# One gate form for all tokens, left-over rows through a scratch tensor, and a table that places the work

## The chip, the cores and the metric

The kernel runs on one core of a Trainium2 chip. That core has five engines with instruction queues of their own: TensorE (PE, matmuls; its weight loads are shown apart as PEld), VectorE (DVE), ScalarE (ACT), GpSimd (POOL) and SyncE (SP), which here issues most DMA transfers. Each queue runs in order; an instruction that waits for another engine holds up what is behind it on its own queue. The metric is the device time of one execution in microseconds.

## The reference

Two parts in a row. Attention packs 576 tokens of each of 8 heads into 32 with `p`, and attends back to them; the result is the input of a feed-forward block with the gate h * erf(softplus(h)).

```
def _attn_ref(q, k, v, p):
    scale = 1.0 / np.sqrt(q.shape[-1])
    def sm_attn(qq, kk, vv):
        s = scale * np.matmul(qq, kk.transpose(0, 1, 3, 2))
        s = s - np.max(s, axis=-1, keepdims=True)
        a = np.exp(s)
        a = a / (np.sum(a, axis=-1, keepdims=True) + 1e-09)
        return np.matmul(a, vv)
    p_packed = sm_attn(p, k, v)
    return sm_attn(q, p_packed, p_packed).astype(np.float32)

def _moe_ref(x, w_in, w_out):
    h = x @ w_in
    sp = np.maximum(h, 0.0) + np.log1p(np.exp(-np.abs(h)))
    g = h * erf(sp)
    return (g @ w_out).astype(np.float32)
```

q, k and v are 8 x 8 x 576 x 64 (batch, heads, tokens, width), p has 32 tokens, w_in is 512 x 2048 and w_out 2048 x 512. The two weights are 64-bit floats, which the kernel turns into 32-bit floats itself by shifting bits.

## The kernel before, in words

The attention's output is never formed. For each batch b the second attention's weights (576 tokens by 8 heads of 32, `a2`) and w' = packed values times w_in (`w_prime`, four blocks j of 512 columns) are made, and h = w' times a2. Float32 operands are split into a high and a low part of type fp32r, and a product is three matmuls (high x high, low x high, high x low).

The work is cut into 128 units (b, f): f is one of 16 blocks of 128 hidden columns. Units go (0, f 0-7), (1, f 0-7), (0, f 8-15), (1, f 8-15), then batches 2 to 7 whole, f 0 to 15. Unit 8 is thus (1, 0), and unit 32 is (2, 0). For a unit:

- `h_block` makes h of 128 columns by 576 tokens in two halves of 288 tokens, six matmuls each (line 308), into PSUM banks of `ps_h`, of which there are two. ScalarE copies each half into `hs` (L311 or L313).
- The gate has two forms. Units 0 to 31 are grouped by three (`gate_group`): Softplus for three units (L286), Erf for three (L289), and a product on VectorE (L291). Softplus, Erf and Exp need different function tables, so a switch costs an ACT_TABLE_LOAD. Units from 32 on use a form of three Tanh and a Square on ScalarE (L321 to L326) and three operations on VectorE (L324 to L327), which share a table with Exp.
- `split_g` makes gh (L272) and gl (L273) on VectorE, two buffers each, and POOL copies the last 64 of the 576 tokens away into `rh` and `rl` (L279).
- `o_block` multiplies with w_out: four blocks of 128 tokens, three matmuls each (L345), summed over f in four PSUM banks. It runs 3 units behind h (5 in the grouped part).
- The 64 left-over tokens of two batches together fill 128 rows; `o_rest` multiplies them in 48 matmuls (L369) once for each pair of batches, from `rh` and `rl`.

The attention of the next batch (twelve stages of a generator, with `ps_m`, a single PSUM buffer), the w' blocks, and the conversions of the weights (`load_f32`: a DMA into one of two staging buffers `wst`, one ScalarE and three VectorE instructions, L92 to L95; w_out is split too, L108 and L109) are put between the units by rules that spread them over a stretch (`plan`). Within what the code issues, a scheduler orders each engine's instructions by its own estimate of time; only the ScalarE functions that need tables are chained in the order written (`in_turn`), and those in the grouped part alone.

## Time and profile before

| what | us |
|---|---|
| three runs: median, lowest, highest | 808.8, 806.19, 4030.56 |
| the profiled execution, its own time | 806.4 |
| its span, from the first instruction to the last | 804.6 |
| mean granted TensorE clock, share of full | 0.949 |

The profile is of one execution. A row of a group of instructions gives its line, engine, operation, output <- inputs, shapes and count, then the busy time, the mean of one in ns, and the idle time of the engine just before them with what ended it. A row of a stretch gives its bounds, its length, each engine's busy time with the count of instructions, the granted clock, the DMA share and GB/s. In the timeline and the chain of waits a row starts with its start and its length. Since matmuls are pipelined, the busy time of one (393 ns for 512 columns) is longer than its share of the queue: twelve in a row take 2.74 us.

### The profile page before, as it was taken

To read this page: it belongs to the slowest core of one execution; us is meant where nothing else is said; L and a number is where in the kernel's file an instruction comes from. 1 tells how busy PE (TensorE), PEld (TensorE's weight loads), DVE (VectorE), ACT (ScalarE), POOL (GpSimd) and SP (SyncE) were. 2 spreads that over 40 slices of the span, in tenths; PEclk is the share of its full clock that TensorE was granted. 3 is DMA by queue.
4 is the path that set the end of the run, shared out by engine and by line. 5 is a ranking of instruction groups with operands and counts; after the bars stand their busy time and mean duration, and the time that the engine had idled before them with its cause. 6 is when DMAs were issued, how large, how long until landed. Compare 5 with 4: busy or idle time off the path is not lost.

```text
span 804.6 us, 12933 instructions
## 1 busy us (share of the span) xinstructions
PE 742.4 (92%) x5008; PEld 579.1 (72%) x5008; DVE 575.8 (72%) x876; ACT 578.1 (72%) x938; POOL 132.2 (16%) x270
## 2 busy tenths in 40 slices
PE   4458738999999999999999999999999999999996
PEld 1237505878867787778877786778877786878885
DVE  3787697845476558978797559777797559768654
ACT  3369367968577767879697657889697658878764
POOL 0002101211031212211211021112221021211101
PEclk8569957999999999999999999999999999999999
DMA  9633543202240512002300321011400310000002
GB/s 309 235 124 107 179 145 126 100 1 102 75 110 1 102 53 93 1 6 97 132 1 1 115 75 58 0 60 43 132 1 3 110 60 1 1 27 28 1 1 66
DMA packets 26685, 57.98 MB, mean 72 GB/s; under 512 B 3072, under 2 KB 4096, under 8 KB 26624
## 3 DMA queue, kind: packets, MB, share of 16 engines
q1 hardware_dynamic: 25472, 55.06, 20.8%
q0 software_dynamic: 1152, 2.10, 1.6%
q8 instruction: 39, 0.64, 0.3%
q14 instruction: 22, 0.18, 0.1%
HBM read 45.61 MB, written 11.53 MB: 71 GB/s over the span
## 4 chain that ended last, share of the span: by engine, by line
PE 83%; DMA 6%; DVE 6%; ACT 4%; issue 1%; SPq 0%; DVEq 0%; ACTq 0%
PE o L345 42%; PE h L308 25%; PE or L369 5%; PE wp L258 5%; DMA wi<-w_in 2%; PE p L213 2%; DMA v<-v 2%; PE s L180 1%; PE s L227 1%; DMA wos<-w_out 1%; PE t L201 1%; DVE wo L94 1%; DVE wpl L261 1%; DVE wo L95 1%; DVE w_in_sb L94 0%
## 5 line engine op out<-in xcount | busy, mean ns | idle before, releaser
L345 PE MATMUL o<-woh,gl 128*128 128x512 f32 x512 | 201.2, 393 | 0.0
L345 PE MATMUL o<-wol,gh 128*128 128x512 f32 x512 | 200.7, 392 | 0.0
L345 PE MATMUL o<-woh,gh 128*128 128x512 f32 x512 | 173.1, 398 | 0.4 <-DVE gh L272 0.4
L308 PE MATMUL h<-a2h,wph 128*128 128x288 f32 x512 | 158.5, 310 | 12.3 <-ACT hs L311 8.3
L308 PE MATMUL h<-a2h,wpl 128*128 128x288 f32 x512 | 153.5, 300 | 0.0
L308 PE MATMUL h<-a2l,wph 128*128 128x288 f32 x512 | 153.4, 300 | 0.0
L279 POOL CAST rh<-gh 128x64 fp32r<-128x64 f32 x128 | 61.7, 483 | 531.8 <-DVE gh L272 531.8
L308 PEld LDWEIGHTS h<-a2h,wph 128*128 128x128 f32 x512 | 97.8, 191 | 47.0 <-ACT hs L311 10.3
L313 ACT ACTIVATE hs<-h 128x288 f32<-128x288 f32 x192 | 75.7, 406 | 71.8 <-PE h L308 68.4
L345 PEld LDWEIGHTS o<-woh,gh 128*128 128x128 f32 x512 | 93.7, 189 | 29.7 <-issue 4.8
L345 PEld LDWEIGHTS o<-woh,gl 128*128 128x128 f32 x512 | 96.1, 188 | 21.1 <-DVE t L325 1.8
L345 PEld LDWEIGHTS o<-wol,gh 128*128 128x128 f32 x512 | 96.1, 188 | 20.3 <-issue 2.2
L327 DVE SCALAR_TENSOR_TENSOR hs<-t,hs 128x576 f32<-128x576 f32 x96 | 72.5, 755 | 49.6 <-ACT t L326 48.5
L273 DVE TENSOR_TENSOR gl<-hs,gh 128x576 fp32r<-128x576 f32 x128 | 101.0, 789 | 7.3 <-POOL rh L279 0.5
L308 PEld LDWEIGHTS h<-a2l,wph 128*128 128x128 f32 x512 | 98.2, 192 | 7.2 <-DVE a2l L248 1.9
L308 PEld LDWEIGHTS h<-a2h,wpl 128*128 128x128 f32 x512 | 98.1, 192 | 2.7 <-issue 2.6
L326 ACT ACTIVATE t<-t,bias 128x576 f32<-128x576 f32 x96 | 74.1, 772 | 32.5 <-DVE t L325 32.1
L272 DVE CAST gh<-hs 128x576 fp32r<-128x576 f32 x128 | 58.3, 456 | 53.6 <-PE o L345 48.3
L324 DVE SCALAR_TENSOR_TENSOR t<-t,hs 128x576 f32<-128x576 f32 x96 | 72.0, 751 | 19.9 <-ACT u L323 19.7
L279 POOL CAST rl<-gl 128x64 fp32r<-128x64 f32 x128 | 64.8, 507 | 116.6 <-DVE gl L273 91.4
L321 ACT ACTIVATE t<-hs,bias 128x576 f32<-128x576 f32 x96 | 74.9, 780 | 2.2
L322 ACT ACTIVATE t<-t,bias 128x576 f32<-128x576 f32 x96 | 74.5, 776 | 2.0
(74 smaller groups left out, 926.7 us busy)
## 6 DMA issues: line engine op xcount, KB each, us to landing
k<-kT SPq DMA_DIRECT2D x32, 288.0 KB, 4.2
q<-qT SPq DMA_DIRECT2D x32, 288.0 KB, 4.4
wi<-w_in SPq DMA_DIRECT2D x16, 512.0 KB, 4.8
v<-v SPq DMA_DIRECT2D x32, 256.0 KB, 4.0
wos<-w_out SPq DMA_DIRECT2D x16, 512.0 KB, 3.8
out<-ob SPq DMA_DIRECT2D x32, 256.0 KB, 2.2
out<-ob POOLq DMA_DIRECT2D x8, 256.0 KB, 5.7
v<-v SPq DMA_DIRECT2D x8, 128.0 KB, 4.2
```

Source lines behind the costliest of these rows:

```text
L258: nc.tensor.matmul(ps[NK * c:NK * c + NK, r, :], pt[b][64 * r:64 * r + 64, NK * c:NK * c + NK], w_in_sb[64 * r:64 * r + 64, c, j * FB:(j + ...
L272: nc.vector.tensor_copy(ghi[:], hs[:])
L273: nc.vector.tensor_tensor(glo[:], hs[:], ghi[:], op=ALU.subtract)
L279: nc.gpsimd.tensor_copy(kept[:, f % PER, b % 2, :], g[:, NTB * P:S])
L308: nc.tensor.matmul(ps[:, 0:HT], w[:, r, fo:fo + P], a[:, r, at_c], start=(m == 0), stop=(m == 5))
L313: nc.scalar.mul(hs[:, at_c], ps[:, 0:HT], 0.5)
L321: nc.scalar.activation(t[:], hs[:], AF.Tanh, bias=bias[:, 0:1], scale=2.0 * T_SCALE)
L322: nc.scalar.activation(t[:], t[:], AF.Square, bias=bias[:, 1:2], scale=Q_SCALE)
L324: nc.vector.scalar_tensor_tensor(t[:], t[:], 0.5 * A2, hs[:], op0=ALU.mult, op1=ALU.add)
L326: nc.scalar.activation(t[:], t[:], AF.Tanh, bias=bias[:, 3:4], scale=2.0 * A_SCALE)
L327: nc.vector.scalar_tensor_tensor(hs[:], t[:], 1.0, hs[:], op0=ALU.add, op1=ALU.mult)
L345: nc.tensor.matmul(acc[b][x][:], gg[:, x * P:(x + 1) * P], w[:], start=(first and n == 0), stop=(last and n == 2))
```

## The change

- The gate has one form, Softplus and Erf, for all 128 units, in groups of four (three near the start and at the end in other sizes: `ends`). All table functions, Exp of the attention too, are chained in the order written. The program has 86 table loads in place of 28.
- POOL's copies of the left-over tokens go. Each gh and gl is stored by a DMA on SP into `rest`, a tensor in device memory (128 rows of 256 bytes), and `o_rest` loads a block of 512 KB of it into a staging buffer `wst` for every 12 matmuls. gh and gl have three buffers.
- A table (`PLAN`) says behind which unit each stage of the attention, each w' block and each conversion stands. h comes in halves with half of another unit's o between them; o is due `wait` units behind the end of its group, one unit's o for each unit of h.
- From unit 48 on, each TensorE instruction is chained to the one before (`pe`), so TensorE runs in program order.
- At the start, the first block of w_in comes in two loads of 1 MB into a part of `w_in_sb` that is not used yet, maxima and Exp of batch 0 read PSUM directly, and batch 1's p, k, v and q are loaded ahead of the second block of w_in, into buffers of w_out among others.

```diff
+PLAN = {
+    "att": {1: (1, 1, 2, 2, 3, 4, 4, 5, 5, 7, 7), 2: (15, 15, 19, 19, 20, 20, 22, 24, 25, 25, 25, 27, 28, 30)},
+    "steady": (0, 0, 0, 1, 2, 2, 5, 6, 7, 9, 11, 11, 12, 13),
...
+    "ends": (4, 5, 8, 12, 13, 16),
+    "wait": (4, 1, 1, 1, 1),
+    "strict": 48,
+}
...
+    def pe(ins):
+        if strict[0] and pe_last:
+            tc.add_manual_dep(ins.ins, pe_last[-1], mybir.DependencyInfo(
+                mybir.DependencyClass.NoSync, mybir.DependencyReason.DATA), reason="order")
+        pe_last[:] = [ins.ins.name]
...
     def split_g(hs, b, f):
...
-        for kept, g in zip(rest[pair, k], (ghi, glo)):
-            nc.gpsimd.tensor_copy(kept[:, f % PER, b % 2, :], g[:, NTB * P:S])
+        for x, g in enumerate((ghi, glo)):
+            nc.sync.dma_start(rest[b // 2, f // PER, :, x, f % PER, b % 2, :], g[:, NTB * P:S].bitcast(F32))
...
-    def h_block(b, f, n):
+    def h_part(n, c):
...
-            if grouped:
-                nc.scalar.copy(hs[:, at_c], ps[:, 0:HT])
-            else:
-                nc.scalar.mul(hs[:, at_c], ps[:, 0:HT], 0.5)
+        nc.scalar.copy(hs[:, at_c], ps[:, 0:HT])
+        if c == 0:
             return
-        nc.scalar.activation(t[:], hs[:], AF.Tanh, bias=bias[:, 0:1], scale=2.0 * T_SCALE)
-        nc.scalar.activation(t[:], t[:], AF.Square, bias=bias[:, 1:2], scale=Q_SCALE)
-        nc.scalar.activation(u[:], t[:], AF.Tanh, bias=bias[:, 2:3], scale=U_SCALE)
-        nc.vector.scalar_tensor_tensor(t[:], t[:], 0.5 * A2, hs[:], op0=ALU.mult, op1=ALU.add)
-        nc.vector.scalar_tensor_tensor(t[:], u[:], 0.5 * A1, t[:], op0=ALU.mult, op1=ALU.add)
-        nc.scalar.activation(t[:], t[:], AF.Tanh, bias=bias[:, 3:4], scale=2.0 * A_SCALE)
-        nc.vector.scalar_tensor_tensor(hs[:], t[:], 1.0, hs[:], op0=ALU.add, op1=ALU.mult)
+        group.append((hs_of.pop(n), b, f))
+        if n + 1 in ends:
+            gate_group()
+            closed.append(n)
...
     def o_rest(pair, k):
...
-        g = rest.pop((pair, k))
+        g = spool.tile([P, 2, PER, 2 * TAIL], F32R, name=f"g{pair}_{k}", tag="wst")
+        nc.sync.dma_start(g[:].bitcast(F32), rest[pair, k].rearrange("p x i two t -> p x i (two t)"))
...
+    for m, (b, f, first, last) in enumerate(units):
+        wait = PLAN["wait"]
+        sent_at = max(sent_at + 1, close[m] + wait[min(m // G, len(wait) - 1)])
+        here = parts.setdefault(min(sent_at, N + m), [])
+        here += [(o_part, (b, f, first, last, x)) for x in (1, 2, 3, 0)]
+        if b % 2 and f == NF - 1:
+            here += [(o_rest, (b // 2, k)) for k in range(NFB)]
+    for n in range(N + NF):
+        strict[0] = n >= PLAN["strict"]
+        here = parts.get(n, [])
+        some = (len(here) + 1) // 2
+        if n < N:
+            h_part(n, 0)
+        for block, what in here[:some]:
+            block(*what)
+        if n < N:
+            h_part(n, 1)
+            do(plan.pop(n, []))
+        for block, what in here[some:]:
+            block(*what)
```

Three places show how instructions move. A name like gl0_7 is gl of batch 0, f 7; wi3_2 is the staged w_in block of columns 3, rows 2; the last number is only a mark of the program.

VectorE around gl of batch 0's unit 7, before:

```order
L291 TENSOR_TENSOR hs0_6_789<-t0_6_935,hs0_6_789 128x576
L95 SCALAR_TENSOR_TENSOR w_in_sb_87<-wi3_3_1041,w_in_sb_87 128x512
L291 TENSOR_TENSOR hs0_7_865<-t0_7_937,hs0_7_865 128x576
L272 CAST gh0_6_945<-hs0_6_789 128x576
L291 TENSOR_TENSOR hs1_0_918<-t1_0_939,hs1_0_918 128x576
L93 TENSOR_SCALAR wo12_1106<-wo12_1106 128x512
L272 CAST gh0_7_952<-hs0_7_865 128x576
L273 TENSOR_TENSOR gl0_6_946<-hs0_6_789,gh0_6_945 128x576
L94 SCALAR_TENSOR_TENSOR wo12_1106<-wos12_1107,wo12_1106 128x512
L273 TENSOR_TENSOR gl0_7_953<-hs0_7_865,gh0_7_952 128x576
```

Here the conversions of the weights' later blocks are ahead of the gates of units 6 and 7. The same place in the changed kernel:

```order
L317 TENSOR_TENSOR gl0_5_788<-hs0_5_659,gh0_5_787 128x576
L317 TENSOR_TENSOR gl0_6_795<-hs0_6_690,gh0_6_794 128x576
L285 TENSOR_REDUCE mx1_687<-ta1_647 128x36
L93 SCALAR_TENSOR_TENSOR w_in_sb_83<-wi2_1_876,w_in_sb_83 128x512
L94 SCALAR_TENSOR_TENSOR wo7_713<-wos7_714,wo7_713 128x512
L307 TENSOR_TENSOR wpl1_0_725<-wp1_0_726,wph1_0_724 128x1024
L316 CAST gh0_7_801<-hs0_7_750 128x576
L286 TENSOR_SCALAR mx1_687<-mx1_687 128x36
L94 SCALAR_TENSOR_TENSOR w_in_sb_83<-wi2_1_876,w_in_sb_83 128x512
L120 TENSOR_TENSOR wol7_721<-wo7_713,woh7_720 128x512
L317 TENSOR_TENSOR gl0_7_802<-hs0_7_750,gh0_7_801 128x576
```

Before, the last conversions of w_in (wi3_3) and a third of those of w_out's second half (wo12) stand ahead of the gates of units 6 and 7; afterwards those gates stand behind wo7 and the second part of wi2, and the rest of w_in comes behind them:

```order
L94 SCALAR_TENSOR_TENSOR w_in_sb_83<-wi2_3_986,w_in_sb_83 128x512
L92 TENSOR_SCALAR w_in_sb_83<-w_in_sb_83 128x512
L93 SCALAR_TENSOR_TENSOR w_in_sb_83<-wi3_0_992,w_in_sb_83 128x512
L94 SCALAR_TENSOR_TENSOR w_in_sb_83<-wi3_0_992,w_in_sb_83 128x512
L307 TENSOR_TENSOR wpl0_2_1114<-wp0_2_1115,wph0_2_1113 128x1024
L92 TENSOR_SCALAR w_in_sb_83<-w_in_sb_83 128x512
L93 SCALAR_TENSOR_TENSOR w_in_sb_83<-wi3_1_1037,w_in_sb_83 128x512
L94 SCALAR_TENSOR_TENSOR w_in_sb_83<-wi3_1_1037,w_in_sb_83 128x512
L92 TENSOR_SCALAR w_in_sb_83<-w_in_sb_83 128x512
L93 SCALAR_TENSOR_TENSOR w_in_sb_83<-wi3_2_1107,w_in_sb_83 128x512
L94 SCALAR_TENSOR_TENSOR w_in_sb_83<-wi3_2_1107,w_in_sb_83 128x512
L92 TENSOR_SCALAR wo8_1195<-wo8_1195 128x512
```

These rows, also VectorE's, stand in the changed kernel between the second half of batch 1's attention and the first gate of batch 1: four conversions in a row.

ScalarE in the full part, around the end of unit 8 of batch 3, before:

```order
L313 ACTIVATE hs3_8_3782<-h3_8_0_3783 128x288
L326 ACTIVATE t3_7_3742<-t3_7_3742,bias_86 128x576
L313 ACTIVATE hs3_8_3782<-h3_8_1_3791 128x288
L321 ACTIVATE t3_8_3799<-hs3_8_3782,bias_86 128x576
L322 ACTIVATE t3_8_3799<-t3_8_3799,bias_86 128x576
L323 ACTIVATE u3_8_3800<-t3_8_3799,bias_86 128x576
L326 ACTIVATE t3_8_3799<-t3_8_3799,bias_86 128x576
```

The functions of one unit follow each other there, and no table load is among them. And afterwards at unit 3 of batch 4, where a group ends (rows L354 are copies of h out of PSUM, L327 is Softplus, L330 Erf, L234 Exp of the next batch):

```order
L354 COPY hs4_3_4073<-h4_3_0_4074 128x288
L354 COPY hs4_3_4073<-h4_3_1_4088 128x288
L327 ACTIVATE t4_3_4102<-hs4_3_4073 128x576
L330 ACT_TABLE_LOAD
L330 ACTIVATE t4_0_4096<-t4_0_4096 128x576
L330 ACTIVATE t4_1_4098<-t4_1_4098 128x576
L330 ACTIVATE t4_2_4100<-t4_2_4100 128x576
L330 ACTIVATE t4_3_4102<-t4_3_4102 128x576
L234 ACT_TABLE_LOAD
L234 ACTIVATE a1_5_4013,sm5_4015<-a1_5_4013,m5_4014 128x576 x2
L354 COPY hs4_4_4142<-h4_4_0_4143 128x288
L354 COPY hs4_4_4142<-h4_4_1_4157 128x288
```

Before, a unit's copies stand between single functions; now four Erf and the two Exp of batch 5 with their table loads stand between the copies of unit 3 and those of unit 4.

The left-over tokens, before, on POOL, a copy for each gh and gl of batch 3:

```order
L279 COPY rh1_2_2883<-gh3_9_3852 128x64
L279 COPY rl1_2_2884<-gl3_9_3853 128x64
L279 COPY rh1_2_2883<-gh3_10_3896 128x64
L279 COPY rl1_2_2884<-gl3_10_3897 128x64
L279 COPY rh1_2_2883<-gh3_11_3940 128x64
L279 COPY rl1_2_2884<-gl3_11_3941 128x64
```

Each tail goes to a tile that the matmuls read later. And afterwards on SP around the left-over matmuls of batches 2 and 3:

```order
L320 DMA rest<-gh4_2_4123 128x64
L384 DMA out<-ob3_15_0_4249 128x512
L320 DMA rest<-gl4_2_4124 128x64
L395 DMA g1_2_4300<-rest 128x1024
L395 DMA g1_3_4314<-rest 128x1024
L407 DMA out<-obr1_4328 64x512 x2
L165 DMA q1_5_3978<-qT 128x576
L165 DMA q2_5_3980<-qT 128x576
L165 DMA q3_5_3982<-qT 128x576
```

The copies on POOL are gone; SP stores the tails, and loads the blocks g2 and g3, of which each waits for the matmuls on the block two before it, ahead of the left-over output and of q for batch 5.

## What the change should do to the time

> **What bounds the kernel now.** I read the page first: the engines' busy shares and the row of the granted clock.
>
> ```profile
> span 804.6 us, 12933 instructions
> PE 742.4 (92%) x5008; PEld 579.1 (72%) x5008; DVE 575.8 (72%) x876; ACT 578.1 (72%) x938; POOL 132.2 (16%) x270
> PE   4458738999999999999999999999999999999996
> PEclk8569957999999999999999999999999999999999
> ```
>
> The reader is to see two parts. From the eighth slice on TensorE is full at the whole clock until the last slice; before that it is half idle. Next came the busy time by stretches: length, then busy us and instructions of PE, PEld, DVE, ACT and POOL, then clock, DMA share and GB/s; and the same for the matmuls of L308 (h) and of L345 (o) alone, up to 140 us.
>
> ```profile
> 80.00:100.00 20.00, 15.83 (x151) 11.92 (x149) 13.76 (x27) 7.02 (x15) 2.48 (x6) 0.96 0.54 180
> 100.00:120.00 20.00, 6.12 (x58) 1.38 (x66) 18.44 (x28) 12.13 (x15) 0.00 (x0) 0.50 0.42 139
> 120.00:140.00 20.00, 17.27 (x87) 10.86 (x86) 15.52 (x25) 13.63 (x23) 2.28 (x4) 0.69 0.40 129
> 160.00:790.00 630.00, 629.85 (x4230) 501.38 (x4229) 453.62 (x672) 478.62 (x777) 115.86 (x236) 1.00 0.16 48
> ...
> 0.00:140.00 140.00, 29.16 (x144) 24.71 (x144) 0.72 0.53 175
> 0.00:140.00 140.00, 20.78 (x81) 15.36 (x82) 0.72 0.53 175
> ```
>
> Of 630 us in the middle TensorE is idle 0.15 us. Up to 140 us it has done 144 of 1,536 h matmuls and 81 of 1,536 o matmuls, 12 of 128 units' h and under 7 units' o. The chain of waits, in order of time, gives the pace of the full part (start, us, what):
>
> ```profile
> 241.86 1.02 PE wp L258 x16
> 268.79 11.11 PE or L369 x48
> 283.16 1.59 PE h L308 x12
> 308.31 2.74 PE o L345 x12
> ```
>
> A unit costs 1.59 + 2.74 = 4.33 us of TensorE, a w' block 1.02, the left-over rows of two batches 11.11. So the kernel is bound by TensorE from about 137 us on, and by what feeds it before. The change leaves the count of matmuls of every kind as it is (1,536 of h, 1,536 of o, 192 of left-over rows); it can win only in the first 137 us, and lose anywhere by new holes.
>
> **What goes from ScalarE and VectorE behind unit 32.** Rows of the groups by line (busy, mean ns, idle before and its releaser):
>
> ```profile
> L291 DVE TENSOR_TENSOR hs<-t,hs 128x576 f32<-128x576 f32 x32 | 23.1, 754 | 25.7 <-ACT t L289 25.7
> L272 DVE CAST gh<-hs 128x576 fp32r<-128x576 f32 x128 | 58.3, 456 | 53.6 <-PE o L345 48.3 <-issue 1.1
> L327 DVE SCALAR_TENSOR_TENSOR hs<-t,hs 128x576 f32<-128x576 f32 x96 | 72.5, 755 | 49.6 <-ACT t L326 48.5
> L321 ACT ACTIVATE t<-hs,bias 128x576 f32<-128x576 f32 x96 | 74.9, 780 | 2.2
> L313 ACT ACTIVATE hs<-h 128x288 f32<-128x288 f32 x192 | 75.7, 406 | 71.8 <-PE h L308 68.4
> L286 ACT ACT_TABLE_LOAD x11 | 14.1, 1283 | 0.2
> L273 DVE TENSOR_TENSOR gl<-hs,gh 128x576 fp32r<-128x576 f32 x128 | 101.0, 789 | 7.3 <-POOL rh L279 0.5
> L279 POOL CAST rh<-gh 128x64 fp32r<-128x64 f32 x128 | 61.7, 483 | 531.8 <-DVE gh L272 531.8
> ```
>
> For each of 96 units four functions of 0.78 become two of 0.69, and three vector operations of 0.755 become one of 0.754: VectorE saves 1.51 us a unit. ScalarE goes from 2 x 0.406 + 4 x 0.78 = 3.9 us to 0.8 + 1.4 and a quarter of two table loads (0.64), about 2.8 us. Both are under the 4.33 us of TensorE before and after, so I put this at nothing: TensorE's full row is the cover. The 256 POOL casts go (POOL waits 531.8 us for VectorE; nobody waits long for it), at nothing too. In their place come 256 stores and 16 loads on SP's queue, 8.4 MB each way over a DMA share of 0.16; a gh/gl buffer is held until its store has landed, but there are three, and o of a unit now comes seven units behind its h (unit 0 is sent at 3 + 4 = 7, then one each), so the group's chain, 6 to 7 us from the last h to gl, stands behind three units or 13 us of TensorE. Also nothing.
>
> **The start.** The same matmuls, 162 of h and 96 of o, stand ahead of the first o of unit 8 (batch 1, f 0) in both orders, so the time of that point compares cleanly. VectorE's part in it, and the end of the wait for its gl:
>
> ```profile
> 67.20:145.60 78.40, 61.27 (x103) 0.78 0.43 141
> ...
> 144.81 0.75 DVE L273 TENSOR_TENSOR gl<-hs,gh 128x576 fp32r<-128x576 f32 x1
> ```
>
> By the order, ahead of that gl the changed kernel has one w_in conversion less, five w_out conversions with their splits less, one w' split less, one gate product and one cast more. Rows:
>
> ```profile
> L94 DVE SCALAR_TENSOR_TENSOR wo<-wos,wo 128x512 uint32<-128x512 uint32 x16 | 10.9, 689 | 0.2
> L109 DVE TENSOR_TENSOR wol<-wo,woh 128x512 fp32r<-128x512 f32 x16 | 10.9, 685 | 1.4 <-ACT woh L108 1.2
> L93 DVE TENSOR_SCALAR wo<-wo 128x512 uint32<-128x512 uint32 x16 | 6.6, 420 | 5.0 <-ACT wo L92 4.9
> L261 DVE TENSOR_TENSOR wpl<-wp,wph 128x1024 fp32r<-128x1024 f32 x32 | 38.9, 1214 | 10.0 <-ACT wph L260 9.8
> L92 ACT ACTIVATE w_in_sb<-wi 128x512 f32<-128x512 f32 x16 | 10.7, 666 | 28.8 <-DMA wi<-w_in 28.8
> ```
>
> A conversion is 0.42 + 2 x 0.69 = 1.80 us of VectorE. So 1.80 + 5 x (1.80 + 0.685) + 1.21 - 0.75 - 0.46 = 14.2 us less. Not all of it is won. The conversions wi2_2 to wi3_2 and wos8 now stand in a row, with two staging buffers, and their loads stand on SP behind four stores of batch 0's first output. By the DMA issues (KB each, us to landing):
>
> ```profile
> wi<-w_in SPq DMA_DIRECT2D x16, 512.0 KB, 4.8
> wos<-w_out SPq DMA_DIRECT2D x16, 512.0 KB, 3.8
> ```
>
> A buffer turns in 4.8 + 0.67 + 1.80 = 7.3 us; six conversions on two buffers take 21.8 us, and VectorE's work in those rows is 17.2 us: 4.6 us go back to waiting. That leaves -9.6 us. From below: VectorE's own 17.1 us of idleness in the 78.4 us above may shrink as well; with half of it the gain is 14.2 + 8.5 = 22.7 us. From above: batch 1's k, v and q (3.5 MB) are now loaded ahead of the second w_in block and w_out, and DMA is already the slow part of the first 40 us; the start could be 5 us later. I take -9.6, the middle that the rows carry.
>
> **New holes in the full part.** First, the left-over rows. Their 48 matmuls now read tiles loaded from the scratch tensor through the two staging buffers. The third load waits for the first 12 matmuls (2.78 us), lands 3.8 us and some 0.2 of hand-over later (the w_out row, the same 512 KB), and only the second 12 matmuls (2.78) cover it: 1.2 us of hole. In program order this stands whole at batches 2-3, 4-5 and the last: 3 x 1.2 = 3.6 us; with the w_in row's 4.8 it is 6.6; split up by other matmuls it would be 0. Behind that wait on SP stand the stores of the left-over output, q1 to q3 of the next batch and the next stores; q is needed three units later, so the 12 us are hidden.
>
> Second, ScalarE at the end of a group. The timeline of such a group before (start, us, instruction):
>
> ```profile
> 198.86 0.40 ACT L311 COPY hs<-h 128x288 f32<-128x288 f32 x1 [0.27 <-PE h L308]
> 199.29 0.69 ACT L286 ACTIVATE t<-hs 128x576 f32<-128x576 f32 x1
> 200.00 1.28 ACT L289 ACT_TABLE_LOAD   x1
> 201.29 1.83 ACT L289 ACTIVATE t<-t 128x576 f32<-128x576 f32 x3
> 203.03 0.35 ACT L208 COPY a1t<-p 64x256 f32<-64x256 f32 x1
> ```
>
> Copy 0.43, Softplus 0.71, load 1.29, four Erf of 0.58: 4.75 us. After unit 3 of a batch the order puts a third load and the next batch's two Exp (0.77 each, by L189) ahead of the copy of unit 4: 4.75 + 1.29 + 1.54 + 0.41 = 8.0 us. TensorE, in program order, has o half, h half, o half, h half, w', o half = 3 x 1.37 + 2 x 0.79 + 1.02 = 6.7 us before it needs that bank of ps_h: a hole of 1.3 us, in four batches 5.2. At the other groups the slack is 2 us or about zero (12th unit). From below 0, if the table's order makes up for it; from above 1.3 at every one of 20 groups, 26 us.
>
> ```profile
> L189 ACT ACTIVATE a<-a,m 128x576 f32<-128x576 f32 x16 | 12.4, 782 | 2.2 <-DVE m L186 2.2
> ```
>
> Here the Trainium skill speaks against the change: ScalarE: Activation LUTs, section "What ACT_TABLE_LOAD costs", gives about 1283 ns for the load plus about 1380 ns of drain, some 2.66 us for each switch of set. The trace agrees with the first figure (1283) and not with the second: Softplus at 199.29 and the load at 200.00 touch, and Erf follows 1.29 us after the load began. By the page's sum the chain above would be 8.0 + 2 x 1.38 = 10.8 us and my four holes 16 us instead of 5.2.
>
> **The sum.** 806.4 us of the profiled execution (span 804.6) - 9.6 + 3.6 + 5.2 = 805.6 us. The end stays: TensorE runs full to the last matmul in both, with seven units of o and the left-over rows behind the last h. The median of the three runs, 808.8, is 0.3% above that execution.
>
> **Rivals.** (1) Faster: the start wins 22.7 us and the holes close, since ScalarE and VectorE have 1.1 and 1.5 us a unit to spare: 806.4 - 22.7 = 784 us. For it: VectorE is idle 22% of 67 to 146 us while TensorE starves, and conversions of w_out that nobody needs yet leave that stretch. Against: ScalarE waits 28.8 us for w_in loads there, and those stay. (2) Slower, by program order: TensorE no longer steps around a late ScalarE, and the bank of the next h is copied behind four Erf at each of 20 groups. A plain group has 2 us of slack; from a delay of 3.2 us on, each group has the 1.2 us of hole that makes 2% (24 us, less what the start wins). At 1.7 us a hole it ends at 805.6 + 20 x 1.7 - 5.2 = 834 us, or 828 with half of that in the attention's groups alone. For it: a table load in every half group; against: 630 us without a hole under the old order. (3) A switch of tables that occupies ScalarE longer than its load when it follows other work: with 1.4 us more per switch the groups with Exp have 16 us and those of the 12th unit some 11 us of hole, 806.4 - 9.6 + 3.6 + 27 = 827 us. It is the page's rule as a mechanism; the touching rows above speak against it. (4) The new place of the left-over rows does nothing: that is already in the sum, since POOL is off the path.
>
> **Chances.** Sum as forecast, start's gain given back: 0.54. Rival 1: 0.30. Rival 2: 0.12. Rival 3: 0.04. "Within 2%" is about what a measurement of this kernel can tell from no change, 16 us; so faster 0.30, same 0.54, slower 0.16. The range takes in rival 1's time and most of rival 2's and 3's: 784 to 826 us.
>
> **What the changed profile would show.** TensorE full from about 127 us instead of 137, and gl of batch 1's first unit ending near 136 us; a wait of TensorE for g of 1 to 2 us behind the first 24 left-over matmuls, three times; a wait of h for the copy of the unit before at every batch's fifth unit, near 1.3 us; 86 table loads of 1.28 us without idle time behind them; POOL nearly idle. I am wrong if TensorE fills before 115 us or after 140, if holes in the full part sum to more than 15 us, or if its rate per unit leaves 4.33 us.

## The result, and the profile after

The changed kernel takes 793.7 us, the median of four runs from 792.9 to 795.3, against 807.7 us for the kernel before: a ratio of 0.9835 with a 95% interval of 0.9806 to 0.9864. It is faster by 1.65%, inside the 2% that was set as "no change". The forecast was 805.6 us, 12 us too high, with a range from 784 to 826. One of the four runs of the kernel before took 4,030.6 us; it is counted in the median and not in the ratio.

The profiled execution took 795.3 us. Its page, with the rows that answer to those of before (span; busy time, share and instructions of each engine; busy tenths and granted clock in 40 slices):

```profile
span 793.4 us, 12893 instructions
PE 733.5 (92%) x5008; PEld 577.0 (73%) x5008; DVE 435.5 (55%) x678; ACT 494.9 (62%) x802; POOL 8.0 (1%) x14
PE   3458978999999999999999999999999999999997
PEclk7568988999999999999999999999999999999999
```

The reader is to see that TensorE does the same 5,008 matmuls with 8.9 us less of busy time (742.4 before), and that VectorE, ScalarE and POOL have lost 140, 83 and 124 us of work of which the time shows almost nothing. Where TensorE stands by stage (columns as in the same view of before):

```profile
80.00:100.00 20.00, 18.92 (x117) 13.43 (x119) 18.72 (x32) 12.02 (x17) 0.00 (x0) 0.95 0.49 153
100.00:120.00 20.00, 14.88 (x84) 7.59 (x84) 15.07 (x22) 11.61 (x19) 0.00 (x0) 0.87 0.58 185
120.00:140.00 20.00, 16.95 (x86) 13.15 (x86) 15.20 (x27) 17.93 (x30) 0.00 (x0) 0.87 0.32 93
324.00:790.00 466.00, 455.58 (x3053) 370.31 (x3051) 227.93 (x348) 286.88 (x462) 0.00 (x0) 0.95 0.23 68
```

Between 100 and 120 us TensorE is busy for 14.88 us where it had 6.12: that is the start. Its granted clock, the third figure from the end, is 0.87 there where it was 0.50. The last row is the surprise. From 324 us, where unit 48 begins in the changed kernel, to 790 us TensorE sat idle for 10.4 us, 1.4 of them behind its last matmul, which ends at 788.6 us, and 9.0 in holes. (The granted clock of 0.95 belongs to this one execution; the second profile of the same kernel, below, has 1.00 there and a span only 0.9 us shorter.) The kernel before, in the same stretch, was idle for 0.15 us:

```profile
324.00:790.00 466.00, 465.85 (x3098) 373.13 (x3097) 355.65 (x523) 361.69 (x592) 86.61 (x170) 1.00 0.13 41
```

So the holes came, as forecast, and yet the changed kernel loses nothing there. What TensorE waits for from 324 us on (waits in total, times, longest):

```profile
PE h L352 <- ACT hs L354: 5.4, 8, 1.2
PE p L258 <- ACT a1t L253: 2.1, 4, 0.5
PE or L398 <- DMA g<-rest: 1.5, 3, 0.5
```

**An account by matmuls.** The trace has the start of each matmul. Give each the time from its start to the next one's start, and put what exceeds its kind's own pace by over 0.55 us under holes. Behind unit 48 the two kernels then read so (us, with the number of unbroken runs in brackets):

```
                     h      o      left-over  w'          s1        s2        p     t, pt   holes
before             132.8  231.7   32.7       24.1 (24)   8.7 (14)  6.4 (8)  10.3   3.7     0.6
after              131.1  245.8   33.4       18.9 (18)   5.3 (8)   5.3 (8)  10.3   4.1    10.0
```

The o matmuls are 992 before and 1,044 after (0.2336 and 0.2354 us each), the w' blocks 17 and 18, because the two orders put a few of them on different sides of unit 48; the other counts are equal. With that in mind w' is cheaper by 17 x (1.42 - 1.05) = 6.3 us, s1 by 3.4, s2 by 1.1 and h by 1.7, 12.5 us in all; o, the left-over matmuls and the transposes are dearer by 3.0 and the holes by 9.4. It comes out even.

**An account by units.** Take the start of the first h matmul of a unit, less the time that all matmuls ahead of it would take without a break (h 0.132 us, o 0.228, left-over 0.230, and fixed amounts, the same for every kernel: about 1.75 us for a w' block and 8.9 for a batch's attention). What is left is TensorE's backlog. The fixed amounts are longer than unbroken runs take (a w' block takes 1.02), so the level says little, and only differences between kernels are read.

```
unit           4     8     12    16    24    48    end
before        43.0  64.8  74.3  73.9  73.1  73.9  73.4
after         41.5  49.6  55.4  61.2  62.4  64.4  63.6
```

At unit 12 the changed kernel is 18.9 us ahead, at unit 16 12.7, at unit 48 9.5, and it stays there. (With 1.02 us for a w' block the lead is 19.0 us at unit 12, 13.4 at unit 16, 10.2 at unit 48 and 9.8 at the end.) From the start of the last matmul to the end of the span it needs 5.2 us instead of 6.5, since one copy and two small stores stand behind the last left-over matmul. Together 9.5 + 0.3 + 1.3 = 11.1 of the 11.2 us between the spans (804.6 and 793.4).

### The profile page after: what moved, and what is told of

Same layout as the page of the kernel before. It is cut to its first block, busy times and chain, and to the rows that moved or that the text cites. A ratio compares the mean times of both kernels' runs of the same rounds, so it can differ in the third digit from the quotient of the medians.

```text
span 793.4 us, 12893 instructions
## 1 busy us (share of the span) xinstructions
PE 733.5 (92%) x5008; PEld 577.0 (73%) x5008; DVE 435.5 (55%) x678; ACT 494.9 (62%) x802; POOL 8.0 (1%) x14
## 4 chain that ended last, share of the span: by engine, by line
PE 71%; ACT 11%; DMA 8%; DVE 6%; issue 2%; SPq 1%; DVEq 0%; ACTq 0%
PE o L374 37%; PE h L352 21%; PE or L398 5%; DMA v<-v 3%; DMA wi<-w_in 3%; PE wp L304 3%; ACT t L330 2%; PE p L258 2%; ACT L330 2%; ACT t L327 1%; ACT hs L354 1%; DMA g<-rest 1%; PE s L272 1%; ACT L327 1%; PE s L209 1%
## 5 line engine op out<-in xcount | busy, mean ns | idle before, releaser
L374 PE MATMUL o<-woh,gh 128*128 128x512 f32 x512 | 201.4, 403 | 1.6 <-ACT ob L379 1.1
L354 ACT COPY hs<-h 128x288 f32<-128x288 f32 x256 | 97.6, 398 | 168.5 <-PE h L352 167.3
L352 PE MATMUL h<-a2h,wph 128*128 128x288 f32 x512 | 155.4, 304 | 14.0 <-ACT hs L354 14.0
L332 DVE TENSOR_TENSOR hs<-t,hs 128x576 f32<-128x576 f32 x128 | 91.8, 754 | 114.1 <-ACT t L330 114.1
L374 PEld LDWEIGHTS o<-woh,gh 128*128 128x128 f32 x512 | 95.6, 188 | 43.1 <-issue 26.9
L317 DVE TENSOR_TENSOR gl<-hs,gh 128x576 fp32r<-128x576 f32 x128 | 96.3, 754 | 2.3
L327 ACT ACTIVATE t<-hs 128x576 f32<-128x576 f32 x128 | 88.0, 687 | 2.8
L330 ACT ACTIVATE t<-t 128x576 f32<-128x576 f32 x128 | 78.1, 675 | 0.4
L304 PE MATMUL wp<-w_in_sb,pt 64*32 64x512 f32 x512 | 47.9, 642 | 4.8 <-DVE wpl L307 3.3
L307 DVE TENSOR_TENSOR wpl<-wp,wph 128x1024 fp32r<-128x1024 f32 x32 | 39.1, 1222 | 17.8 <-ACT wph L306 17.2
```

The lines of the kernel that those rows point to most:

```text
L304: pe(nc.tensor.matmul(ps[NK * c:NK * c + NK, r, :], pt[b][64 * r:64 * r + 64, NK * c:NK * c + NK], w_in_sb[64 * r:64 * r + 64, c, j * FB:( ...
L307: nc.vector.tensor_tensor(lo[:], ps[:], hi[:], op=ALU.subtract)
L317: nc.vector.tensor_tensor(glo[:], hs[:], ghi[:], op=ALU.subtract)
L327: in_turn(nc.scalar.activation(t[:], hs[:], AF.Softplus))
L330: in_turn(nc.scalar.activation(t[:], t[:], AF.Erf))
L332: nc.vector.tensor_tensor(hs[:], t[:], hs[:], op=ALU.mult)
```

## The experiments

Twelve kernels ran, each beside the kernel before. Theory A says that TensorE pays for every unbroken run of matmuls on parts of the array (w', s1, s2, p; "row-tiled"), however many matmuls it holds, and that program order pays for its holes by breaking up fewer of them. Rival B says that such runs cost nothing extra and that holes are made up elsewhere. "The base" is the changed kernel in the first of these runs.

### The changed kernel again

> The changed kernel once more, as the base for the three that follow. Theory A (TensorE pays about 0.85 us each time it enters and leaves a run of row-tiled matmuls, w', s1, s2 or p; program order cut those runs behind unit 48 from 50 to 38, and that paid for the new holes) and rival B (the runs cost nothing extra, the holes are made up elsewhere, and the gain is the start's alone): both the same as the first measurement, 794 us or 0.983 of the kernel before.

Measured: 793.4 us, ratio 0.9828 (0.9815 to 0.9841). This is the base of what follows.

### Program order taken away

```diff
-    "strict": 48,
+    "strict": 1 << 30,
```

> Program order taken away (strict from a unit that never comes); the scheduler places TensorE's work again, and its order has 55 row-tiled runs behind unit 48 instead of 38. Theory A: 17 runs more cost 17 x 0.85 = 14.5 us, the holes of 5.3 + 3.2 + 2.0 = 10.5 us close at most: 794 + 4 = 798 us, between 794 and 808. Rival B: the holes close and the runs cost nothing: about 784 us. The second rival of the prediction (program order makes TensorE wait) also expects about 784 us.

Measured: 795.2 us, ratio 0.9858 (0.9841 to 0.9876), 1.8 us above the base: the holes are gone and the kernel is no faster. TensorE's stretch, in which its last matmul ends at 787.7 us, leaves no idle time up to there:

```profile
324.00:790.00 466.00, 463.74 (x3028) 369.67 (x3026) 226.88 (x346) 284.14 (x459) 0.00 (x0) 1.00 0.23 68
```

Its rows between 397 and 402 us on TensorE (start, us, instruction, count) show why:

```profile
398.19 1.04 PE L304 MATMUL wp<-w_in_sb,pt 64*32 64x512 f32 x2
399.16 0.40 PE L352 MATMUL h<-a2h,wph 128*128 128x288 f32 x1
...
400.15 1.08 PE L304 MATMUL wp<-w_in_sb,pt 64*32 64x512 f32 x14
401.16 0.50 PE L374 MATMUL o<-woh,gl 128*128 128x512 f32 x1
```

A w' run of 2 matmuls holds TensorE from 398.19 to 399.16, 0.97 us; the run with the other 14 from 400.15 to 401.16, 1.01 us. The scheduler had split the block to fill a wait, and the block cost twice. The kernel before does the same (a block in pieces of 4, 8 and 2), against a whole block of 16 at 402.25 us:

```profile
402.25 1.09 PE L258 MATMUL wp<-w_in_sb,pt 64*32 64x512 f32 x16
403.27 0.40 PE L308 MATMUL h<-a2h,wph 128*128 128x288 f32 x1
...
495.26 1.05 PE L258 MATMUL wp<-w_in_sb,pt 64*32 64x512 f32 x4
496.24 0.40 PE L308 MATMUL h<-a2h,wph 128*128 128x288 f32 x1
...
497.23 1.06 PE L258 MATMUL wp<-w_in_sb,pt 64*32 64x512 f32 x8
498.22 1.20 PE L345 MATMUL o<-woh,gh 128*128 128x512 f32 x4
499.35 1.04 PE L258 MATMUL wp<-w_in_sb,pt 64*32 64x512 f32 x2
500.32 0.40 PE L308 MATMUL h<-a2h,wph 128*128 128x288 f32 x1
```

Start to next start: 1.02 us for 16, 0.98 for 4, 0.99 for 8, 0.97 for 2. The single records behind these rows show why a short run is hardly cheaper. A matmul of w' is two records, and each works on a part of the array (64x32). The 16 records at 402.25 us start in two lots of eight, 7 ns apart within a lot and 0.45 us from lot to lot: eight parts work side by side. The 2 records at 398.19 us start 0.45 us apart as well, and the other parts stand empty. A split block loses this working side by side.

By the account by matmuls, free order behind unit 48 has 25 w' runs (25.0 us) and 16 s2 runs (9.9 us) where the base has 18 (18.3) and 8 (5.2): 11.4 us more, against 10.2 us of holes that went. The 784 us of rival B are ruled out; theory A's 798 us had each of the 17 runs at 0.85 us, and they cost 0.67, since eight of them are s2 runs of 0.6 us and two are runs of p, which took 0.2 us more in all.

### w' in two halves

```diff
         for c in range(NC):
+            if c == NC // 2 and b > NB0:
+                yield
             for r in range(2):
                 pe(nc.tensor.matmul(ps[NK * c:NK * c + NK, r, :], pt[b][64 * r:64 * r + 64, NK * c:NK * c + NK],
...
         for block, what in here[some:]:
             block(*what)
+            while halved:
+                next(halved.pop(), None)
```

> Program order kept, but each w' block of batches 3 to 7 is issued as two halves of 4 matmul pairs with one o block of 3 matmuls between them: 17 row-tiled runs more behind unit 48 (55 instead of 38), same matmuls, same holes. Theory A: + 17 x 0.85 = 14.5 us, 808 us (804 to 812). Rival B: no change, 794 us within 1.5.

Measured: 809.5 us, ratio 1.0031 (1.0017 to 1.0044): 16.1 us above the base, which is theory A's side, with the same matmuls and program order throughout. The first block on TensorE that is split:

```profile
347.25 1.06 PE L306 MATMUL wp<-w_in_sb,pt 64*32 64x512 f32 x8
348.24 0.51 PE L376 MATMUL o<-woh,gh 128*128 128x512 f32 x1
348.58 0.40 PE L376 MATMUL o<-woh,gl 128*128 128x512 f32 x1
...
349.14 1.06 PE L306 MATMUL wp<-w_in_sb,pt 64*32 64x512 f32 x8
350.14 0.50 PE L376 MATMUL o<-woh,gh 128*128 128x512 f32 x1
```

Each half takes 0.99 us, and the o matmul behind it 0.34 us to the next instead of 0.23. One thing was not foreseen: in this trace TensorE no longer waits for the copies of h at all. The longer w' gives ScalarE the time that it lacked, so the four holes of 1.3 us are inside the 16.1 us: the 17 extra runs cost (16.1 + 5.3) / 17 = 1.26 us each by the medians. By the account by matmuls it is 1.17: w' takes 16.5 us more than in the base, and the o matmuls around it 3.4.

### Exp behind the copies

```diff
-    "steady": (0, 0, 0, 1, 2, 2, 5, 6, 7, 9, 11, 11, 12, 13),
+    "steady": (0, 0, 0, 1, 2, 2, 4, 6, 7, 9, 11, 11, 12, 13),
...
+        if b > NB0:
+            functions.append(copies[-1])
...
-        nc.scalar.copy(hs[:, at_c], ps[:, 0:HT])
+        copies[:] = [nc.scalar.copy(hs[:, at_c], ps[:, 0:HT]).ins.name]
```

> From batch 3 on the two Exp of the attention are put behind the two copies of h of the batch's fifth unit, instead of straight behind the Erf of the group. Theory A: the four holes of 1.3 us on TensorE at the fifth unit go, and nothing takes their place: 794 - 5.3 = 788.7 us (787 to 791). Rival B: the holes are slack that is made up later, or the Exp delays the next copies as much: 794 us within 1.5.

Measured: 789.1 us, ratio 0.978 (0.9764 to 0.9796), 4.3 us below the base. In the changed kernel ScalarE's timeline at such a unit reads so:

```profile
344.25 1.28 ACT L330 ACT_TABLE_LOAD   x1
345.55 2.41 ACT L330 ACTIVATE t<-t 128x576 f32<-128x576 f32 x4
347.98 1.28 ACT L234 ACT_TABLE_LOAD   x1
349.27 0.78 ACT L234 ACTIVATE a<-a,m 128x576 f32<-128x576 f32 x1
...
350.81 0.68 ACT L354 COPY hs<-h 128x288 f32<-128x288 f32 x2
```

and TensorE's, with the wait in brackets:

```profile
349.66 0.39 PE L374 MATMUL o<-wol,gh 128*128 128x512 f32 x1
351.23 0.40 PE L352 MATMUL h<-a2h,wph 128*128 128x288 f32 x1 [1.18 <-ACT hs L354]
```

The copy that the h at 351.23 needs stands behind the load for Exp and two Exp. With the copies first, the waits of h for copies fall from 5.6 us in the base to 2.2 in eight pieces of at most 0.3. The hole was real time.

### p one unit later

```diff
-    "steady": (0, 0, 0, 1, 2, 2, 5, 6, 7, 9, 11, 11, 12, 13),
+    "steady": (0, 0, 0, 1, 2, 2, 5, 6, 7, 8, 9, 11, 11, 12, 13),
...
         nc.scalar.copy(a1t[0:REM, NT].rearrange("p r k -> p (r k)"), pr[0:REM, 0:2 * P])
+        if b > NB0:
+            yield
```

> From batch 3 on the p stage is split: the two transposes and ScalarE's copy of their result stay where they are, the 40 p matmuls come one unit later. Theory A: the four holes of 0.80 us, in which p waits for that copy, go: 793.4 - 3.2 = 790.2 us (789 to 791.5). Rival B (such a hole is made up elsewhere): 793.4 within 1.

Measured: 792.5 us, ratio 0.9825 (0.9798 to 0.9851): 0.9 us below the base and not to be told from it. The four waits for a1t are gone, and two new ones have come. TensorE's timeline at one of them:

```profile
551.47 0.69 PE L274 MATMUL s<-q,pt 64*32 64x288 f32 x8
552.91 0.43 PE L274 MATMUL s<-q,pt 64*32 64x288 f32 x2 [0.75 <-DMA q<-qT]
```

v, k and q share six buffers, so with p a unit later v is held a unit longer and q can be loaded only later; this is read from the code and was not tried by itself. The first s2 half takes 1.88 us in one batch and 2.77 in another instead of 0.65. That is 3.4 us lost against some 2.7 won. Rival B's number, but for another reason: the hole was not made up elsewhere, it was exchanged.

### Left-over matmuls in two pieces

```diff
-        here += [(o_part, (b, f, first, last, x)) for x in (1, 2, 3, 0)]
+        todo = [(o_part, (b, f, first, last, x)) for x in (1, 2, 3, 0)]
+        if first and b >= NB0 and b % 2 == 0:
+            todo[3:3] = [(o_rest, (b // 2 - 1, k)) for k in (2, 3)]
         if b % 2 and f == NF - 1:
-            here += [(o_rest, (b // 2, k)) for k in range(NFB)]
+            todo += [(o_rest, (b // 2, k)) for k in ((3,) if b == B - 1 else (0, 1))]
+        if b == B - 1 and f in (NF - 3, NF - 2):
+            todo += [(o_rest, (b // 2, k)) for k in ((0, 1) if f == NF - 3 else (2,))]
+        here += todo
```

> The 48 left-over matmuls of a pair of batches no longer stand in one piece: the first 24 behind the pair's last unit, the other 24 one unit later, behind three o blocks of the next batch; at the last pair 24, 12 and 12 behind the last three units. Theory A: the three holes of 0.61 to 0.69 us before the third load's matmuls go: 793.4 - 2.0 = 791.4 us (790.5 to 792.5); four more changes from o to left-over matmuls cost nothing, as both use the whole array. Rival B: 793.4 within 1.

Measured: 794.3 us, ratio 0.9845 (0.982 to 0.9869), not below the base. The waits for g are gone; in their place:

```profile
PE or L398 <- ACT ob L379: 2.0, 2, 1.0
PE o L374 <- ACT obr L404: 1.4, 2, 0.7
```

In the new places no half of h lies between the last o on a bank and the first left-over matmul on it, nor between the last left-over matmul and the next o: 3.4 us of waits for ScalarE's copies instead of 1.6 us of waits for loads.

### VectorE's start made heavier

```diff
-        nc.vector.scalar_tensor_tensor(bits, high, 0x80000000, bits, op0=ALU.bitwise_and, op1=ALU.bitwise_or)
-        nc.vector.scalar_tensor_tensor(bits, low, 29, bits, op0=ALU.logical_shift_right, op1=ALU.bitwise_or)
+        for _ in range(2 if again else 1):
+            nc.vector.scalar_tensor_tensor(bits, high, 0x80000000, bits, op0=ALU.bitwise_and, op1=ALU.bitwise_or)
+            nc.vector.scalar_tensor_tensor(bits, low, 29, bits, op0=ALU.logical_shift_right, op1=ALU.bitwise_or)
...
-        nc.vector.tensor_tensor(lo[:], wo[f][:], hi[:], op=ALU.subtract)
+        for _ in range(2 if 1 <= f <= 7 else 1):
+            nc.vector.tensor_tensor(lo[:], wo[f][:], hi[:], op=ALU.subtract)
```

(`again` is true for the w_out blocks 1 to 7)

> Seven of the early w_out conversions do their last two vector operations and their split's subtraction twice, with the same values. By the order, VectorE's work ahead of gl of unit 8 grows by 10 x 0.69 + 7 x 0.685 - 0.84 - 0.75 = 10.1 us. Theory A (the start's end is set by VectorE's work, as the prediction's start term has it): 793.4 + 10 = 803 us, 799 to 805. Rival (the loads or ScalarE set the start's end, and the 9.8 us came from the loads' new order): 793.4 to 796.

Measured: 809.3 us, ratio 1.0041 (1.0024 to 1.0059), 15.9 us above the base, past theory A's 805. The backlog by units:

```
unit             4     8     12    16    24    48    end
base            43.4  50.1  56.3  62.1  63.2  64.7  62.7
start_loaded    40.2  54.8  63.2  66.9  70.4  75.7  75.2
```

From unit 4 to unit 12 it grows by 23.0 us instead of 12.9: 10.1 us more; against all ten profiles with the unloaded start it is 8.7 to 10.1 us more, which is about what VectorE was given. The rest comes between units 16 and 48 (8.8 us instead of 2.6). The order had also pushed two conversions behind gl of unit 8; that these are what comes due there is argued, not shown.

### The old gate from unit 32 on

```diff
+        if n >= 2 * NF:
+            t = tpool.tile([P, S], F32, name=f"t{b}_{f}", tag="t0")
+            u = tpool.tile([P, S], F32, name=f"u{b}_{f}", tag="t1")[:]
+            nc.scalar.activation(t[:], hs[:], AF.Tanh, bias=bias[:, 0:1], scale=2.0 * T_SCALE)
...
+        if n >= 2 * NF:
+            grouping[0] = False
+            split_g(hs, b, f, n)
```

> From unit 32 on the old gate of three Tanh and a Square, unit by unit, in the changed kernel's places and program order: ScalarE does about 1.1 us and VectorE 1.5 us more a unit, and some 60 table loads of 1.28 us go. Theory A (the gates are off the path, only the chain at a group's end makes holes): the 5.3 us of holes at the fifth units go and no others come, 793.4 - 5 = 788 us (786 to 793). Rival (the relief of ScalarE and VectorE is part of the gain): above 800 us.

Measured: 1,057 us, ratio 1.31 (1.306 to 1.314): a miss of 269 us, and not for the gate's work. TensorE waits 188.1 us for the copies of h, in 77 pieces. The group of these copies (busy, mean ns, idle ahead of it and its releaser):

```profile
L377 ACT ACTIVATE hs<-h 128x288 f32<-128x288 f32 x192 | 69.2, 406 | 170.4 <-DVE gl L337 162.0
```

o comes seven units behind its h, and gh has three buffers, so gl of a unit waits for the o of the unit three ahead of it, four units later; hs had eight buffers in the changed kernel (two names of four) and only four here, since u took the other four. The copies then wait for gl. The seven units' distance is paid for in buffers, and the run says nothing on the gate.

The same with a distance of three units:

```diff
-        sent_at = max(sent_at + 1, close[m] + wait[min(m // G, len(wait) - 1)])
+        if m < 26:
+            sent_at = max(sent_at + 1, close[m] + wait[min(m // G, len(wait) - 1)])
+        else:
+            sent_at = max(m + 3, 33 + (m - 26) // 2)
```

> The old gate from unit 32 on as in the run before, but o of a unit comes three units behind its h instead of seven, so that three buffers of gh and four of hs are enough. Theory A (the gates' work on ScalarE and VectorE is off the path as long as the buffers fit the distance): the four holes at the fifth units go, 788 us (785 to 796). Rival (with the old gate ScalarE is too full for program order): above 800 us.

Measured: 794.1 us, ratio 0.9841 (0.9823 to 0.986), not to be told from the base. ScalarE is busy for 565.8 us and VectorE for 569.7 where the base has 494.3 and 435.3, and no h waits for a copy. But the left-over matmuls wait longer for g (4.8 us instead of 1.6), as there is less time between their stores and them, and o waits 2.6 us for gh and gl:

```profile
PE or L428 <- DMA g<-rest: 4.8, 3, 2.5
PE o L404 <- DVE gl L337: 2.1, 3, 1.0
```

The gates' work itself is off the path, as priced; the 788 us expected were not reached, because the shorter distance made new waits.

### The kernel before, in program order

```diff
+        strict[0] = n >= 48
         if n < len(units):
             grouping[0] = n < GROUPED
```

(every matmul and transpose goes through the same `pe` as in the changed kernel)

> The kernel before with one edit: TensorE in program order from unit 48, without the table's places. The row-tiled runs behind unit 48 go from 50 to 33: seven runs of w' at 0.98 us, six of s1 at 0.61, so 6.9 + 3.7 = 10.6 us less. But the old code puts wp, t1 and p back to back on one bank, and s2_0 and s2_1 too, and in order TensorE stands still for the copies between them: about 2.4 + 1.2 + 0.6 + 1.5 = 5.7 us in each of four batches, 23 us. Theory A: 807 - 10.6 + 23 = 819 us (811 to 827): program order pays only with the table's places. Rival (order alone pays): 796 us.

Measured: 837.4 us, ratio 1.0372 (1.035 to 1.0395). Program order without the table's places costs 3.7%, and the time lies past theory A's range, 811 to 827 us. The waits of TensorE behind unit 48:

```profile
PE t L210 <- DVE wpl L270: 15.9, 4, 4.9
PE p L216 <- ACT a1t L162: 5.4, 4, 2.1
PE s L236 <- DVE ta L239: 4.4, 4, 1.1
```

and five windows around the first of them (TensorE's granted clock is the third figure from the end):

```profile
360.00:365.00 5.00, 5.00 (x48) 4.05 (x40) 4.02 (x8) 4.97 (x10) 0.95 (x3) 1.00 0.58 187
365.00:370.00 5.00, 0.85 (x16) 0.00 (x0) 4.03 (x8) 4.78 (x10) 0.80 (x1) 1.00 0.60 225
370.00:375.00 5.00, 2.73 (x13) 1.88 (x14) 2.74 (x4) 3.67 (x6) 0.00 (x0) 0.52 0.00 0
375.00:380.00 5.00, 5.00 (x81) 4.79 (x82) 0.48 (x2) 0.00 (x0) 0.00 (x0) 0.50 0.54 170
380.00:385.00 5.00, 5.00 (x18) 4.02 (x17) 0.40 (x1) 0.00 (x0) 0.00 (x0) 0.61 0.40 130
```

t waits for w' on its one bank, p for t, s2 for s2: 27.5 us with p's wait for a1t (1.8), not far from the 23 expected. The other part is the clock: after 4.9 us without a matmul TensorE is granted half its clock for over 10 us (10.2 to 13.7 in the four batches), and p takes 4.55 us instead of 2.57.

### Three mends together

The Exp behind the copies as above; the two transposes ahead of p half a unit earlier, with p where it was; and the left-over matmuls in two pieces, with a half of h behind the first four blocks:

```diff
+    half = {first_use[b] - NF + 7: [("att", b)] for b in range(NB0 + 1, B)}
...
             h_part(n, 0)
+            do(half.pop(n, []))
...
+            todo[2:2] = [(o_rest, (b // 2 - 1, k)) for k in (2, 3)]
...
-        some = (len(here) + 1) // 2
+        some = 4 if any(it[0] is o_rest for it in here) else (len(here) + 1) // 2
```

> The changed kernel with three mends behind unit 48: Exp behind the copies of the fifth unit (- 4.3 us, as measured alone); the two transposes ahead of p half a unit earlier, with p and so the loads of q where they were (4 x 0.6 = - 2.4 us); the left-over matmuls in two pieces with the halves of h between them and the copies they wait for (three holes of 0.7, - 2.0 us). Theory A: 793.4 - 8.7 = 784.7 us (783 to 787). Rival (each mend makes a new wait, as the run with p one unit later and the run with the spread left-over rows did): 789 us, the first mend alone.

Measured: 783.8 us, ratio 0.9716 (0.9699 to 0.9733): 9.6 us below the base, and the best of all kernels here. From 324 us on TensorE waits for nothing but copies of h, 2.2 us in eight pieces. Its stretch up to where its matmuls end, at 777.5 us:

```profile
324.00:780.00 456.00, 451.32 (x3038) 370.13 (x3030) 227.00 (x347) 285.24 (x461) 0.00 (x0) 1.00 0.23 70
```

TensorE is idle for 2.2 us from 324 to 777.5 us. From the start of unit 48 to its last matmul this trace is 8.4 us shorter than the base's, near the 8.7 expected. The other 1.8 us between the two spans lie in the start, where single profiles of the same start differ by more than that. So the holes were worth their length, once each was closed without opening another.

### Eight subtractions to POOL

```diff
-        nc.vector.tensor_tensor(lo[:], wo[f][:], hi[:], op=ALU.subtract)
+        (nc.gpsimd if f < 8 else nc.vector).tensor_tensor(lo[:], wo[f][:], hi[:], op=ALU.subtract)
```

> The kernel with three mends, and in the start the subtractions of the first eight w_out splits (0.685 us each on VectorE) go to the idle POOL. By the order, VectorE's work ahead of gl of unit 8 changes by - 7 x 0.685 + 2.0 (one conversion more) + 0.46 = - 2.3 us. Theory A (VectorE's work sets the end of the start): 783.8 - 2 = 782 us, up to 5 less if all eight count (779 to 783.5). Rival (POOL, whose cast of 128x64 took 0.483 us in the kernel before, is too slow for 128x512, and o waits for wol; or the loads set the start's end): 784 us or more.

Measured: 790.4 us, ratio 0.981 (0.9782 to 0.9838), 6.6 us slower than without it. POOL's group (busy, mean ns):

```profile
L120 POOL TENSOR_TENSOR wol<-wo,woh 128x512 fp32r<-128x512 f32 x8 | 14.2, 1776 | 82.4 <-ACT woh L119 82.4
```

Seven take 1.26 to 1.39 us and the eighth 5.11, against 0.685 us on VectorE. In the trace the backlog is 3.0 us larger than with the three mends alone at unit 4, 0.6 at unit 12, 3.4 at unit 24 and 5.0 at the end. Which of the late wol and the changed order around it does this stays open: profiles of kernels whose start is the same differ by 3.6 us at unit 4 (39.8 to 43.4). So work added to VectorE in the start costs its length or more, but this attempt to take some away did not pay.

## Why the prediction was off by 12 us

The forecast that the time stays within 2% (chance 0.54) held, and the time lies in the range. But the ratio of 0.9835 is clear of 1, and the forecast of 805.6 us left out a gain that paid for the holes.

**What bounds the kernel.** Right in kind: TensorE in the full part, and before that what feeds it. The full part begins near 130 us, not at 137 (see the start). ScalarE, VectorE and POOL lost 348 us of work together, and the gate was shown to be off the path by the run with the old gate and the shorter distance (794.1 against 793.4).

**The start, - 9.6 us.** The sum was right and its way was not, so the agreement is luck in part. The backlog at unit 48 is 9.5 us smaller (10.2 with 1.02 us for a w' block). But gl of unit 8 came earlier than "near 136 us":

```profile
131.03 0.75 DVE L317 TENSOR_TENSOR gl<-hs,gh 128x576 fp32r<-128x576 f32 x1
```

It ended at 131.8 us, 13.8 before the old kernel's 145.6, nearly the whole 14.2 us of VectorE's work. What is given back comes behind it, and not only from conversions on two staging buffers: 5.8 us of backlog between units 12 and 16, of which the largest piece is a group's end on ScalarE.

```profile
129.07 0.40 PE L352 MATMUL h<-a2h,wph 128*128 128x288 f32 x1 [3.04 <-ACT hs L354]
```

Behind this hole the granted clock is 0.5 for 3.4 us (from 130.5), some 1.7 us more by an estimate, as half of them is lost. And "TensorE full from about 127 us instead of 137" was wrong, too. The last such hole of the kernel before ends earlier, not later:

```profile
127.26 0.61 PE L308 MATMUL h<-a2h,wph 128*128 128x288 f32 x1 [2.73 <-ACT hs L311]
```

The full part begins 1.8 us later in the changed kernel, with more done by then: at 130 us 162 matmuls of h and 97 of o have started, where it was 114 and 72.

The clock is a part of the start that the prediction did not price. The kernel before has half the clock from 98.4 to 132.5 us, around waits of 4.5 and 7.6 us on TensorE; the changed kernel has it for 3.4 us twice behind 100 us. The run with VectorE's start made heavier shows that VectorE's work counts there. How much of the lead of 18.9 us at unit 12 is clock, and how much comes from the new order of loads, no run separates.

**The left-over rows, + 3.6 us.** The mechanism was right, the size was not: three holes in the foreseen place, 2.0 us together by the account, not 3.6. The load landed in 3.3 us (median), not in the 3.8 of the w_out load that stood in for it.

**ScalarE at the group's end, + 5.2 us.** Right in place and size: four holes of 1.55 us from the last o to h, 1.32 over o's pace, 5.3 us in all; moving Exp won 4.3. The step's bound of zero, "if the table's order makes up for it", did not come.

**A hole that was missing.** TensorE in program order also waits between the two transposes and p for ScalarE's copy: four times 0.80 us from start to start, 2.7 us in all over the transposes' own pace. The prediction went through the stages for ScalarE's queue and not for each pair of matmul blocks that pass data through a copy.

**The step that failed.** "The change leaves the count of matmuls of every kind as it is ...; it can win only in the first 137 us, and lose anywhere by new holes." The count was the wrong measure. Behind unit 48 the old order broke w' and s1 into 24 and 14 runs where 17 and 8 do, and each run costs its 0.6 to 1 us again. With the first h matmuls behind the runs and shorter waits of s2 that is 12.5 us of TensorE's work, and the prediction read the price of w' off an unbroken block only (1.02 us x16) and took the 0.15 us of idle time in the old kernel for proof that nothing could be won there. The runs with halves (+ 16.1 us), free order (+ 11.4 us of runs against - 10.2 us of holes) and the three mends (- 9.6 us) show both sides of the exchange. The Trainium skill has a rule that bears on this, without a price: TensorEngine Tiling (Array Packing), section "Key Properties", says that changing the tiling mode, and not just the tile, drains TensorE. In the traces a change costs little beside the run itself: the last o ahead of a w' run takes 0.32 us and the first behind it 0.34, where o's pace is 0.23. Most of the 0.97 us goes with the columns: 0.60 us for 288 and 0.97 for 512 are 1.65 ns a column, so some 0.85 us for 512, by an estimate from these two.

**The rest of the sum.** 9.1 us of the forecast's error lie behind unit 48 (+ 8.8 forecast, - 0.3 measured), 1.3 in the end ("the end stays" was wrong by that much), and the profiled execution stood 0.2% above its median.

**The rivals.** Rival 1's 784 us were reached, but by the mends and not by the change. Rival 2 named the right mechanism, with the condition that plain groups delay h; h waits 0.2 us at one plain group of a batch and not at the others. Rival 3, 1.38 us more for each switch of tables (ScalarE: Activation LUTs in the Trainium skill, section "What ACT_TABLE_LOAD costs"), is answered by the rows above: Erf ends at 347.96, the load begins at 347.98, Exp at 349.27, and the 85 loads behind the first take 1.283 us each with 1.4 us of idle time ahead of them in all.

## What to carry to other kernels

A full engine is not an engine at its least work: where matmuls on parts of the array stand among full ones, count the unbroken runs, not the matmuls: here the matmuls of a run worked side by side, and a short run lasted as long as a full one. Never let a scheduler split a run to fill a wait that is shorter than the run. A fixed order pays only with a table that gives every hand-over through a copy some other work to stand behind; without the table it cost 3.7%. And when a hole is closed by moving work, follow the buffers and banks of what was moved, for three of the moves here closed a hole and opened another.

## What the runs showed of the hardware that was not expected

- A row-tiled run costs nearly the same whatever its length: w' (64x32 tiles, 512 columns) 0.97 us with 2 matmuls and 1.02 with 16; s1 and s2 (288 columns) 0.60 us with 2 and 0.65 with 16. The records of 16 start in two lots of eight, 0.45 us apart for w'.
- A wait of 4.9 us on TensorE was followed by a granted clock of 0.50 for over 10 us, and a wait of 3.0 us, in the changed kernel at 126 us, by 3.4 us of it, while the base with its holes of 1.3 us has 1.00 from 324 us to the end of its matmuls. The Trainium skill agrees: TensorE: Matmul & The Clock Gate, section "Why this matters for your kernels", warns of idle gaps of over some 3 us.
- A subtraction of two 128x512 tiles on POOL took 1.26 to 1.39 us seven times and 5.11 once. SBUF — State Buffer in the Trainium skill, section "Who interferes with whom", says of the port pair that GpSimd shares with VectorE in its 2-port modes that whoever issues first has it for the whole instruction and the other is blocked; that this was the cause of the 5.11 us is not shown here.
